# q of two early chunks turned in full tiles, their x in rows of tokens, first k and v loads in longer rows

## The chip, the cores and the metric

The kernel runs on one core of one Trainium2 chip. The metric is device time in microseconds (us), the median of several runs; less is better. TensorE multiplies, VectorE and ScalarE work element by element, GpSimd does small odd pieces (here a power), and SyncE issues every DMA.

## What is computed

Attention without softmax, then a two-layer feed-forward product with an odd nonlinearity. There are 8 batches of 8 heads, 576 tokens and 64 values a head; 4608 tokens of width 512 go through the second part, with 2048 hidden units.

```python
kv = np.einsum('bhsd,bhse->bhde', k, v)
out = np.einsum('bhsd,bhde->bhse', q, kv)
rms = np.sqrt(np.mean(out * out, axis=-1, keepdims=True) + 1e-06)
x = (out / rms * g_norm)          # then (tokens, heads * 64)
h = x @ w_in
g = h * np.cos(h)
return (g @ w_out).astype(np.float32)
```

q, k, v and g_norm are 32-bit floats. The two weight matrices come as 64-bit floats, and the kernel itself turns them into 32-bit pairs (a high and a low part).

## The kernel before, in words

The tokens are cut into 9 chunks of 512 (CH), the heads into 4 pairs (p), and the 2048 hidden units into 16 blocks j of 128. For each chunk and each pair a tile x, with the 128 values of the pair on the partitions and 512 tokens beside each other, is made from q and kv; it is split into a high and a low part (xhi, xlo).

A **step** is one chunk and one block j. Its first stage (stage1_part, line 683) makes h in one PSUM bank from four pairs, three products each (xhi with the high and the low weights, xlo with the high ones); act_part (line 708) makes g = h cos h on ScalarE and VectorE and splits it; the second stage (stage2_part, line 744) adds 4 x 3 products with w_out's block to four accumulators (acc0 to acc3). The order of the steps is in `segments` (line 245): chunk 0 with blocks 0 to 4, chunk 1 with blocks 0 to 6, chunk 0 with 5 to 15, chunk 1 with 7 to 15, and then the chunks 2 to 8 whole. What chunks 0 and 1 have added up at the first break goes out to memory and is added again later.

Each weight block (wi j for the first layer, wo j for the second) is loaded once, 512 KB, and converted by w_part (line 629): two or three operations on ScalarE (sg, wi or wo, sometimes m) and three or four on VectorE (m, sg, sg, and the low part). It then stays in its slot of wpool. The slots of the blocks needed last are lent (line 807) to the early loads of k, v and q and to kv_front, the 32-bit kv of batches 0 and 1; the lent block is loaded when the borrower is done.

Chunks 0 and 1 (FRONT = 2) are made in another way than the later ones, in plain 32-bit products:

- kv_loads_front and kv_load (lines 318 to 333) load k and v of a pair to 96 partitions, 6 tokens of 64 values in a row of 1536 bytes. kv_front_part (line 384) makes kv of the pair in 12 products, the two heads in the two halves of the columns, and copies the two 64 x 64 results.
- q_loads_front (line 351) puts q in rows of tokens, four tokens of a head side by side (1 KB a row). x_part (line 450) turns it with eight products by the identity, 64 columns wide (lines 460 to 464).
- chunk 0: four products with q as the stationary operand give x in rows of tokens (line 499); the sum of squares, the power on GpSimd, the scaling (lines 520 to 535), and then four transposes bring x to the needed form (line 537), from which xhi and xlo are read with g_norm as the factor.
- chunk 1: two products give x turned already (line 506), 448 and 64 tokens since the chunk covers two batches. The sums of squares are eight small products with `pair` (line 566), the factors are spread out by ScalarE and turned back by four transposes (line 580).

kv_split_part (line 434) splits batch 1's kv for chunk 2, pair by pair; chunks from 2 on use kv_hi and kv_lo.

The order of instructions on every engine is fixed when the program is made, by the planner `Order` (line 52). Every piece of work yields what it waits for, its cost on an engine and a priority; the planner takes the piece that can start first, and among those the lowest priority. Priorities come from `due(i)` (line 258), a guess at when step i is done. DMA is an engine of the planner with a cost of its own for each load (1.9 for k and v of a pair, 0.85 for q, 1.5 for a weight block), starting at 1.0, and a load counts as landed 2.0 later (DMA_LAT). The loads are issued by SyncE in that order. Engines run strictly in the planned order, so a piece planned too early blocks what stands behind it. The loads of the front and their priorities are in lines 819 to 838:

```python
t = due(begin[c]) - 32 + 3 * p if c else -100.0 + p
load(1.9, t, [kv_in[c, p]], kv_loads_front(c, p, lend(2, [kv_used[c, p]])))
```

Lines 227 to 231 multiply zeros 28 times before any data are there.

Of the kernel before, what the change touches and what calls it, by code (L numbers as in the profile page):

```python
# [19 lines left out]
P = 128  # L20
EPS = 1e-6
# [126 lines left out]
def tile_kernel(  # L148
# [23 lines left out]

    FRONT = 2

# [59 lines left out]
    pair = const.tile([P, 2], F32, name="pair")  # L234
    pool.memset(pair, 0.0)
    for j in range(2):
        pool.memset(pair[j * D:(j + 1) * D, j:j + 1], 1.0)
# [7 lines left out]
    segments = [(0, 0, 5), (1, 0, 7), (0, 5, 16), (1, 7, 16)]  # L245
# [24 lines left out]

# [58 lines left out]
    def kv_loads_front(b, p, tags):  # L329

        def issue():
            kv_load(b, p, *(wpool.tile([P, 2, SI, D], F32, name=f"{kind}{j}") for kind, j in tags))
        return issue
# [17 lines left out]
    def q_loads_front(c, p, tag):  # L351

        def issue():
# [3 lines left out]
            for b, s0, o0, n in chunk_parts(c):  # L357
                nc.sync.dma_start(  # L358
                    out=qn[o0 // NTT:(o0 + n) // NTT, :, :, :],
                    in_=q[b, 2 * p:2 * p + 2, s0:s0 + n, :].rearrange("h (r a) d -> r h a d", a=NTT))  # L360
# [23 lines left out]
    def kv_front_part(b, p, prio):  # L384
        yield "wait", [kv_in[b, p]]
        yield "take", t_psa, prio
        bank = yield "take", t_bank, prio
        _, end = yield "run", [("PE", 1.0)], prio
        ps = ps_tile(bank)
        kt, vt = kv_tiles.pop((b, p))  # L390
        for i in range(SI):
            for j in range(2):
                pe.matmul(
                    out=ps[j * D:(j + 1) * D, 0:D], lhsT=kt[0:SP, j, i, :], rhs=vt[0:SP, j, i, :],
                    start=(i == 0), stop=(i == SI - 1))
        sched.fire(kv_used[b, p], end)
        e, end = yield "run", [("ACT", 0.41, 0.0), ("DVE", 0.45, 0.3)], prio
        for j in range(2):
            r = slice(j * D, (j + 1) * D)
            copy(e, kv_front[r, b, p, j * D:(j + 1) * D], ps[r, 0:D])  # L400
# [33 lines left out]
    def kv_split_part(b, p, prio):  # L434

        yield "wait", [kv_done[b, p]]
        yield "run", [("ACT", 0.29)], prio
        act.copy(out=kv_hi[:, b % 2, p, :], in_=kv_front[:, b, p, :])
        _, end = yield "run", dve_only(P), prio
        dve.tensor_tensor(  # L440
            out=kv_lo[:, b % 2, p, :], in0=kv_front[:, b, p, :], in1=kv_hi[:, b % 2, p, :].bitcast(F32),
            op=ALU.subtract)
        sched.fire(kv_split[b, p], end)
# [6 lines left out]
    def x_part(c, p, prio):  # L450
        yield "wait", [q_in[c, p]]
        front = c < FRONT
        yield "take", t_two, prio
        if front:
            yield "take", t_psa, prio
            bank = yield "take", t_bank, prio
            _, _ = yield "run", [("PE", 0.9)], prio
            qn = q_tiles.pop((c, p))
            ps_t = ps_tile(bank)
            for a in range(NTT):  # L460
                for j in range(2):
                    pe.matmul(
                        out=ps_t[j * D:(j + 1) * D, a * P:(a + 1) * P], lhsT=qn[:, j, a, :], rhs=ident,
                        start=True, stop=True)
        else:
            yield "take", t_qT
            _, end = yield "run", [("DVE", dve_us())], prio
            qT = at.tile([P, CH], F32, name="qT", bufs=1)
            dve.transpose(out=qT, in_=q_tiles.pop((c, p)).rearrange("p a b -> p (a b)"))
            sched.give(t_q, end)  # L470
        if front:
            e, end = yield "run", copiers(), prio
            qT = at.tile([P, CH], F32, name="m")
            copy(e, qT, ps_t[:, 0:CH])
            give_ps(bank, end)
        else:
            yield "run", [("ACT", act_us())], prio
            qhi = at.tile([P, CH], F32R, name="m")
            qlo = at.tile([P, CH], F32R, name="sg")
            act.copy(out=qhi, in_=qT)  # L480
            _, end = yield "run", dve_only(CH), prio
            dve.tensor_tensor(out=qlo, in0=qT, in1=qhi.bitcast(F32), op=ALU.subtract)
            sched.give(t_qT, end)
        parts = chunk_parts(c)
        yield "wait", [kv_done[b, p] if front or b >= FRONT else kv_split[b, p] for b, _, _, _ in parts]
# [6 lines left out]
        pe_us = sum(0.88 * n / 512 if front else 3 * max(0.11, (n + 32) / 2400) for _, _, _, n in parts)  # L492
        _, end = yield "run", [("PE", pe_us)], prio if front else -1.0
        ps = ps_o.tile([P, DM], F32, name=f"acc{acc}") if c == 0 else ps_tile(bank)
        for b, s0, o0, n in parts:
            if c == 0:

                for a in range(NTT):
                    pe.matmul(
                        out=ps[:, a * P:(a + 1) * P], lhsT=qT[:, a * P:(a + 1) * P], rhs=kv_front[:, b, p, :],  # L500
                        start=True, stop=True)
                continue
            if front:
                out_r, q_r = (
                    t[:, 0:CH].rearrange("p (a r) -> p a r", a=NTT)[:, :, o0 // NTT:(o0 + n) // NTT] for t in (ps, qT))
                pe.matmul(out=out_r, lhsT=kv_front[:, b, p, :], rhs=q_r, start=True, stop=True)
                continue
# [11 lines left out]
        if c == 0:  # L519
            heads = lambda t: t.rearrange("p (n d) -> p n d", d=D)  # L520
            yield "run", [("DVE", dve_us())], prio
            ms = small.tile([P, 2 * NTT], F32, name="ms")
            dve.tensor_reduce(out=ms, in_=heads(sq), axis=AX.X, op=ALU.add)
            _, end = yield "run", [("DVE", 0.1)], prio
            sched.give(t_s1, end)
            dve.tensor_scalar(out=ms, in0=ms, scalar1=EPS, scalar2=None, op0=ALU.add)
            yield "run", [("POOL", 1.4)], prio
            rinv = small.tile([P, 2 * NTT], F32, name="rinv")
            pool.tensor_tensor(out=rinv, in0=ms, in1=mhalf[:, 0:2 * NTT], op=ALU.pow)
            yield "take", t_r, prio  # L530
            yield "run", [("DVE", dve_us())], prio
            x = ew.tile([P, CH], F32, name="r")
            dve.tensor_tensor(
                out=heads(x), in0=heads(ps[:, 0:CH]),
# [52 lines left out]
        else:  # L587
# [12 lines left out]
            for e in range(4):  # L600
                act.copy(out=swp[32 * (e ^ 1):32 * (e ^ 1) + 32, :], in_=part[32 * e:32 * e + 32, :])
# [293 lines left out]
```

## Time and profile before

| | us |
|---|---|
| median of 3 runs | 883.26 (881.87 to 884.6) |
| the profiled execution | 880.51 |
| its span, first to last instruction | 878.7 |
| TensorE busy | 866.5 (99%) |
| VectorE busy | 595.1 (68%) |
| ScalarE busy | 509.0 (58%) |
| GpSimd busy | 101.0 (11%) |

The profile is of one execution; its times are microseconds from the start of the span. PE is TensorE's multiplying, PEld its loading of the stationary operand, DVE is VectorE, ACT ScalarE, POOL GpSimd, SP SyncE. Nearly every instruction is recorded by one helper, so all have line 197 (L197), and groups are told apart by tiles: `bank` and `acc` are PSUM, and a tile of wpool shows the name of its slot, so early k, v, q and kv_front appear as `wi` or `wo`. One 32-bit product appears as two records (x8 for four products), one transpose as one. The busy time of products overlaps with the next ones, so that the price of a piece of TensorE work is read from start to start.

### The profile page before, as it was taken

The numbers are of one execution on the slowest core, as the hardware profiler recorded it, in microseconds if no ns is written. First come the engines' busy times: TensorE is split into PE (matmuls) and PEld (weight loads), VectorE is DVE, ScalarE is ACT, GpSimd is POOL, SyncE is SP. The second block draws the span as 40 slices with busy tenths as digits, with TensorE's granted clock in tenths as the row PEclk, the third lists the DMA queues.
The fourth block names the chain that finished last, engine by engine and source line by source line (L and its number), as shares of the span: only waits on it lengthen the run. The fifth ranks groups of instructions, "written<-read, shape, count | busy, mean of one in ns | idle before, by whom it ended". The sixth has DMA issues, their size and how long they took to land.

```text
span 878.7 us, 12282 instructions
## 1 busy us (share of the span) xinstructions
PE 866.5 (99%) x4648; PEld 718.4 (82%) x4648; DVE 595.1 (68%) x973; ACT 509.0 (58%) x972; POOL 101.0 (11%) x49
## 2 busy tenths in 40 slices
PE   7999999999999999999999999999999999999998
PEld 6878888888888888888888888888888888888886
DVE  2888989788677657765766567755766667654553
ACT  3788888556555556455655565545555555545444
POOL 2220000013021102110112011110211012100000
PEclk9999999999999999999999999999999999999999
DMA  9996020471422031302220042203000110001001
GB/s 261 306 366 194 1 73 0 125 192 31 122 44 41 7 90 37 67 13 54 73 67 13 0 115 64 28 1 114 13 13 13 25 48 1 1 1 48 1 1 48
DMA packets 94603, 59.52 MB, mean 68 GB/s; under 512 B 63312, under 2 KB 85840, under 8 KB 94544
## 3 DMA queue, kind: packets, MB, share of 16 engines
q1 hardware_dynamic: 94544, 58.74, 24.6%
q8 instruction: 36, 0.59, 0.3%
q14 instruction: 23, 0.19, 0.1%
HBM read 47.19 MB, written 11.53 MB: 67 GB/s over the span
## 4 chain that ended last, share of the span: by engine, by line
PE 96%; DMA 2%; ACT 1%; SPq 0%; issue 0%; DVE 0%; ACTq 0%
PE bank L197 51%; PE acc L197 45%; DMA wi<-in_moe_w_in_dram 1%; DMA out_dram<-ob 1%; DMA wo<-in_q_dram 1%; ACT ob L197 0%; SPq L320 0%; DVE sg L197 0%; ACT m L197 0%; ACT s L197 0%; DVE r L197 0%; ACT r L197 0%; SPq L358 0%; ACT ghi L197 0%; ACTq L197 0%
## 5 line engine op out<-in xcount | busy, mean ns | idle before, releaser
L197 PE MATMUL acc<-wo,ghi 128*128 128x512 f32 x1152 | 356.6, 391 | 0.2
L197 PE MATMUL bank<-xhi,wi 128*128 128x512 f32 x1088 | 337.8, 392 | 0.7 <-ACT m L197 0.7
L197 PEld LDWEIGHTS acc<-wo,ghi 128*128 128x128 f32 x1152 | 215.1, 188 | 45.7 <-ACT ob L197 0.6
L197 ACT ACTIVATE r<-r 128x512 f32<-128x512 f32 x288 | 181.5, 630 | 118.3 <-DVE r L197 114.8
L197 PEld LDWEIGHTS bank<-xhi,wi 128*128 128x128 f32 x1088 | 202.5, 188 | 42.8 <-ACT m L197 0.9
L197 PE MATMUL acc<-wo,glo 128*128 128x512 f32 x576 | 224.3, 389 | 0.0
L197 PE MATMUL bank<-xlo,wi 128*128 128x512 f32 x544 | 211.9, 389 | 0.0
L197 POOL TENSOR_TENSOR rinv<-ms,mhalf 128x16 f32<-128x16 f32 (+1 forms) x36 | 98.2, 2727 | 658.2 <-DVE ms L197 658.2
L197 DVE SCALAR_TENSOR_TENSOR r<-ki,bank 128x512 f32<-128x512 int32 x144 | 98.7, 685 | 85.5 <-ACT ki L197 84.4
L197 ACT ACTIVATE ki<-bank 128x512 int32<-128x512 f32 x144 | 85.8, 596 | 108.4 <-PE bank L197 106.2
L197 DVE SCALAR_TENSOR_TENSOR r<-r,bank 128x512 f32<-128x512 f32 x144 | 98.6, 685 | 72.4 <-ACT r L197 72.1
L197 PEld LDWEIGHTS acc<-wo,glo 128*128 128x128 f32 x576 | 108.1, 188 | 22.8
L197 DVE TENSOR_TENSOR glo<-r,ghi 128x512 fp32r<-128x512 f32 x144 | 98.3, 683 | 33.3 <-ACT ghi L197 32.4
L197 PEld LDWEIGHTS bank<-xlo,wi 128*128 128x128 f32 x544 | 102.1, 188 | 21.4
L197 ACT CAST ghi<-r 128x512 fp32r<-128x512 f32 x144 | 89.0, 618 | 48.1 <-DVE r L197 47.6
L197 DVE SCALAR_TENSOR_TENSOR r<-ki,r 128x512 f32<-128x512 int32 x144 | 98.7, 685 | 2.3
L197 ACT ACTIVATE s<-bank 128x512 f32<-128x512 f32 x32 | 19.2, 599 | 31.4 <-PE bank L197 31.4
L197 DVE STREAM_TRANSPOSE qT<-s 128x512 f32<-128x512 f32 x28 | 19.9, 710 | 18.7 <-ACT s L197 18.6
L197 DVE STREAM_TRANSPOSE s<-rinv 128x512 f32<-128x512 f32 x28 | 19.8, 708 | 16.3 <-POOL rinv L197 16.3
L197 ACT COPY swp<-part 32x16 f32<-32x16 f32 x112 | 22.6, 202 | 8.3 <-DVE part L197 6.7
L197 ACT CAST xhi<-s 128x512 fp32r<-128x512 f32 x32 | 19.7, 618 | 11.5 <-DVE s L197 11.3
L197 ACT ACTIVATE ob<-acc 128x512 f32<-128x512 f32 x31 | 18.2, 598 | 7.9 <-PE acc L197 5.4
(93 smaller groups left out, 544.8 us busy)
## 6 DMA issues: line engine op xcount, KB each, us to landing
wi<-in_moe_w_in_dram SPq DMA_DIRECT2D x16, 512.0 KB, 9.8
wo<-in_moe_w_out_dram SPq DMA_DIRECT2D x16, 512.0 KB, 8.7
out_dram<-ob SPq DMA_DIRECT2D x31, 256.0 KB, 2.1
kt<-in_k_dram SPq DMA_DIRECT2D x24, 288.0 KB, 4.0
vt<-in_v_dram SPq DMA_DIRECT2D x24, 288.0 KB, 4.6
qb<-in_q_dram SPq DMA_DIRECT2D x32, 48.0 KB, 2.3
wi<-in_k_dram SPq DMA_DIRECT2D x5, 288.0 KB, 6.2
wo<-in_v_dram SPq DMA_DIRECT2D x5, 288.0 KB, 9.2
```

The lines of the kernel that those rows point to most:

```text
L197: return lambda *a, **kw: tc.keep_in_program_order(f(*a, **kw))
```

## The change

1. q of chunks 0 and 1 is seen as tiles of 128 tokens by (two tokens of a head, 64 values) and is turned by four full transposes for a pair of heads instead of eight half-wide products. For that kv_front becomes one tile for each batch, with the kv of every head twice, in both halves of the diagonal (four copies for a pair instead of two).
2. Chunk 1 is made like chunk 0, in rows of tokens: six products (128 columns each) instead of two; two of the six are for the 64 tokens that still belong to batch 0 and write 32 rows. Then the sum of squares on VectorE, the power, the scaling and four transposes, as chunk 0 does. The products with `pair`, the spreading of the factors and their transposes go. x_front_part does this for both chunks; x_part keeps what chunks 2 to 8 need, unchanged. Chunk 1's q is loaded with two tokens in a row (512 bytes) in three pieces, and its output rows follow.
3. k and v of batch 0 are loaded to 128 partitions, 9 tokens in a row (2304 bytes), and multiplied in 9 x 2 products of 64 rows.
4. kv_split_part takes all pairs at once, in two copies and two subtractions.
5. The plan: segments of 4, 8, 12 and 8 steps, other due times, weight loads 4 earlier in priority, a table `haste` that moves single loads and pieces (wo1 and the k and v of pair 1 of batch 1 far ahead, q of pair 0 of chunk 0 behind the other pairs' q, k and v of its pairs 2 and 3 behind that), 34 products with zeros instead of 28, 22 lent slots instead of 21.

```diff
-    for _ in range(28):
+    for _ in range(34):
...
-    segments = [(0, 0, 5), (1, 0, 7), (0, 5, 16), (1, 7, 16)]
+    segments = [(0, 0, 4), (1, 0, 8), (0, 4, 16), (1, 8, 16)]
...
-        return 24.0 + STEP * i + 0.8 * min(i, 14)
+        return 24.0 + STEP * i + 1.6 * min(i, 14)
...
+    def front_rows(c):
+        if c == 0:
+            return [(0, 0, P, 0), (0, 0, P, 1)]
+        return [(1, 0, P, 0), (1, 0, P, 1), (0, 0, (S - CH) // 2, 0)]
...
+            kt, vt = (wpool.tile([P, SF, D], F32, name=f"{kind}{j}") for kind, j in tags)
+            for t, src in ((kt, k), (vt, v)):
+                nc.sync.dma_start(out=t, in_=src[b, 2 * p:2 * p + 2].rearrange("h (p i) d -> (h p) i d", i=SF))
...
+        n = SI if b else SF
+        for i in range(n):
+            for j, r in enumerate(heads):
+                lhs, rhs = (t[0:SP, j, i, :] if b else t[r, i, :] for t in (kt, vt))
+                pe.matmul(out=ps[r, 0:D], lhsT=lhs, rhs=rhs, start=(i == 0), stop=(i == n - 1))
...
+            for r in heads:
+                copy(e, kv_front[b][r, 2 * p + j, r], ps[heads[j], 0:D])
...
+        yield "wait", [kv_done[b, p] for p in range(NP)]
...
+        qn = q_tiles.pop((c, p)).rearrange("p j (m s) d -> p (j m) (s d)", s=2)
+        ps_t = ps_tile(bank)
+        for n in range(NTT):
+            pe.transpose(out=ps_t[:, n * P:(n + 1) * P], in_=qn[:, n, :], identity=ident)
...
+        by_token = ps.rearrange("p (a j d) -> p a j d", j=2, d=D)
+        for b, r0, r1, m in todo:
+            for j in range(2):
+                o = (2 * j + m) * P
+                pe.matmul(
+                    out=by_token[r0:r1, 2 * m:2 * m + 2, j, :], lhsT=qT[:, o + r0:o + r1],
+                    rhs=kv_front[b][:, 2 * p + j, :], start=True, stop=True)
...
-        prio = due(i + 2) - STEP
+        prio = due(i + 2) - 8.0
...
-    lent, slots = {}, sorted(need, key=lambda x: (need[x], x))[-10 * FRONT - 1:]
+    lent, slots = {}, sorted(need, key=lambda x: (need[x], x))[-11 * FRONT:]
...
+    haste = {
+        ("load kv", 0, 2): 2.5, ("load kv", 0, 3): 3.5, ("load kv", 1, 1): -98.4,
+        ("load q", 0, 0): 3.5, ("load q", 1, 2): 10.0,
+        ("load", "wi", 3): 10.0, ("load", "wo", 0): 10.0, ("load", "wo", 1): -130.0,
+        ("kv", 0, 3): -10.0, ("x", 1, 0): -2.0, ("x", 1, 2): -20.0, ("x", 1, 3): -20.0, ("wi", 1): 10.0,
+    }
...
+        (pool if b else dve).memset(kv_front[b], 0.0)
...
+            load(2.4 if c else 1.9, t, [kv_in[c, p]], kv_loads_front(c, p, lend(2, [kv_used[c, p]])))
...
+            load(1.1 if c else 0.85, t, [q_in[c, p]], q_loads_front(c, p, key))
...
-        load(1.5, due(need[key]) - 10, [w_in[key]], w_loads(key), wait=lent.get(key, ()))
+        t = due(need[key]) - 14 + haste.get(("load",) + key, 0.0)
+        load(1.5, t, [w_in[key]], w_loads(key), wait=lent.get(key, ()))
```

The scaling of chunk 1 is the code of chunk 0, lines 515 to 556, with the bank given back at its end.

## Rows read from the trace of the kernel before

**Rows 1.** The page, engine shares: busy us, share of the span, instructions.
```profile
PE 866.5 (99%) x4648; PEld 718.4 (82%) x4648; DVE 595.1 (68%) x973; ACT 509.0 (58%) x972; POOL 101.0 (11%) x49
```

**Rows 2.** The page, chain that ended last, share of the span by engine.
```profile
PE 96%; DMA 2%; ACT 1%; SPq 0%; issue 0%; DVE 0%; ACTq 0%
```

**Rows 3.** Stretches: PE, PEld, DVE, ACT, POOL busy (instructions), granted clock, DMA share, GB/s.
```profile
26.07:62.50 36.43, 35.32 (x286) 27.99 (x284) 29.91 (x57) 29.55 (x59) 6.64 (x4) 1.00 1.03 341
60.00:160.00 100.00, 100.00 (x448) 82.85 (x448) 90.25 (x150) 82.67 (x152) 1.64 (x1) 1.00 0.25 80
```

**Rows 4.** Timeline of TensorE: start, us, engine, operation, out<-in, shapes [idle before].
```profile
15.36 0.92 PE L197 MATMUL bank<-wi,wo 96*64 96x64 f32 x24
19.19 2.08 PE L197 MATMUL acc<-wo,m 128*128 128x128 f32 x8 [2.91 <-ACT m L197]
...
26.07 0.71 PE L197 MATMUL bank<-xhi,wi 128*128 128x512 f32 x2
...
46.71 0.62 PE L197 MATMUL acc<-wo,ghi 128*128 128x512 f32 x2
```

**Rows 5.** Timelines of ScalarE and VectorE: first operation on wi0, low halves of wi0, wo0.
```profile
17.98 0.69 ACT L197 ACTIVATE sg<-wi 128x512 f32<-128x512 f32 x1 [3.81 <-DMA wi<-in_moe_w_in_dram]
...
23.20 0.68 DVE L197 TENSOR_TENSOR wi<-sg,wi 128x512 fp32r<-128x512 f32 x1
...
39.72 0.69 DVE L197 TENSOR_TENSOR wo<-sg,wo 128x512 fp32r<-128x512 f32 x1
```

**Rows 6.** Stretches as in rows 3, about the first big product.
```profile
16.28:19.19 2.91, 0.00 (x0) 0.00 (x1) 1.21 (x3) 1.22 (x3) 0.00 (x0) 0.84 1.11 303
19.19:25.00 5.81, 5.81 (x51) 5.47 (x52) 4.68 (x10) 3.50 (x9) 3.69 (x2) 0.50 1.10 262
```

**Rows 7.** Timeline of TensorE, pieces of the early attention and what follows them.
```profile
9.46 1.16 PE L197 MATMUL acc<-wo,m 128*128 128x128 f32 x8
...
10.55 1.09 PE L197 MATMUL bank<-ident,wo 128*64 128x128 f32 x16
...
29.86 1.14 PE L197 MATMUL bank<-m,wo 128*128 128x64 f32 x4
30.93 1.09 PE L197 MATMUL bank<-ident,wo 128*64 128x128 f32 x16
31.95 0.73 PE L197 MATMUL bank<-kt,wi 128*128 128x512 f32 x2
...
33.44 0.60 PE L197 MATMUL acc<-ident,r 128*128 128x128 f32 x4
33.88 0.95 PE L197 MATMUL bank<-pair,s 128*128 128x2 f32 x8
34.69 0.71 PE L197 MATMUL bank<-xhi,wi 128*128 128x512 f32 x2
...
35.91 0.39 PE L197 MATMUL bank<-vt,wi 128*128 128x512 f32 x1
36.23 0.92 PE L197 MATMUL bank<-wo,wi 96*64 96x64 f32 x24
```

**Rows 8.** Packets in the windows 15 to 20, 45 to 50 and 182 to 190 us.
```profile
DMA packets 1371, 1.51 MB, mean 302 GB/s; under 512 B 78, under 2 KB 1371, under 8 KB 1371
q1 hardware_dynamic: 1371, 1.51, 110.1%
...
DMA packets 1145, 1.90 MB, mean 380 GB/s; under 512 B 59, under 2 KB 889, under 8 KB 1145
q1 hardware_dynamic: 1145, 1.90, 105.9%
...
DMA packets 3076, 1.78 MB, mean 223 GB/s; under 512 B 2258, under 2 KB 2562, under 8 KB 3076
q1 hardware_dynamic: 3076, 1.78, 78.8%
```

**Rows 9.** Groups by shape from 0 to 65 us: count, busy us, mean ns, idle before.
```profile
L197 DVE TENSOR_REDUCE ms<-s 128x8 f32<-128x512 f32 x4 | 2.7, 682 | 10.2 <-ACT s L197 10.2
L197 ACT COPY s<-rinv 128x512 f32<-128x512 f32 x4 | 2.5, 617 | 2.5 <-POOL rinv L197 2.5
L197 ACT COPY wo<-bank 64x64 f32<-64x64 f32 x16 | 3.3, 206 | 4.9 <-PE bank L197 4.5
```

More of the change, by code (lines that the diff above doesn't have):

```diff
@@ L432, in kv_part, with kv_split_part @@
             sched.fire(kv_done[b, p], end)
[L434 to L443, printed above, removed]
+    def kv_split_part(b, prio):
+        yield "wait", [kv_done[b, p] for p in range(NP)]
+        for j in range(2):
+            r = slice(j * D, (j + 1) * D)
+            src = kv_front[b].rearrange("p (n j) d -> p n j d", j=2)[r, :, j, r]
+            yield "run", [("ACT", act_us(NP * D))], prio
+            act.copy(out=kv_hi[r, b % 2, :, r], in_=src)
+            _, end = yield "run", [("DVE", dve_us(NP * D))], prio
+            dve.tensor_tensor(
+                out=kv_lo[r, b % 2, :, r], in0=src, in1=kv_hi[r, b % 2, :, r].bitcast(F32), op=ALU.subtract)
+        for p in range(NP):
+            sched.fire(kv_split[b, p], end)
@@ L446, in x_tokens, with x_front_part @@
     def x_tokens(c, p):
         return t_kv if c == 0 and p >= 2 else t_x
-    def x_part(c, p, prio):
+    def x_front_part(c, p, prio):
         yield "wait", [q_in[c, p]]
-        front = c < FRONT
         yield "take", t_two, prio
[L454 to L485, printed above, removed]
@@ L491, in x_part @@
             bank = yield "take", t_bank, prio
-        pe_us = sum(0.88 * n / 512 if front else 3 * max(0.11, (n + 32) / 2400) for _, _, _, n in parts)
-        _, end = yield "run", [("PE", pe_us)], prio if front else -1.0
+        _, end = yield "run", [("PE", 1.6 if c else 0.95)], prio
         ps = ps_o.tile([P, DM], F32, name=f"acc{acc}") if c == 0 else ps_tile(bank)
-        for b, s0, o0, n in parts:
[L496 to L507, printed above, removed]
+        by_token = ps.rearrange("p (a j d) -> p a j d", j=2, d=D)
@@ new lines, in x_front_part @@
+        yield "run", [("POOL", 1.4)], prio
+        rinv = small.tile([P, 2 * NTT], F32, name="rinv")
+        pool.tensor_tensor(out=rinv, in0=ms, in1=mhalf[:, 0:2 * NTT], op=ALU.pow)
+        yield "take", t_r, prio
+        yield "run", [("DVE", dve_us())], prio
+        x = ew.tile([P, CH], F32, name="r")
+        dve.tensor_tensor(
+            out=heads(x), in0=heads(ps[:, 0:CH]),
+            in1=rinv.rearrange("p (n o) -> p n o", o=1).broadcast_to([P, 2 * NTT, D]), op=ALU.mult)
+        _, end = yield "run", [("PE", 0.5)], prio
@@ new lines, in x_front_part @@
+        for a in range(NTT):
+            pe.transpose(out=ps[:, a * P:(a + 1) * P], in_=x[:, a * P:(a + 1) * P], identity=ident)
+        sched.give(t_r, end)
+        t_slot = x_tokens(c, p)
+        yield "take", t_slot, prio
+        yield "run", [("ACT", act_us() + 0.08)], prio
+        if t_slot is t_kv:
+            xhi, xlo = (
+                kvp.tile([P, 2, SI, D], F32R, name=n).rearrange("p h i d -> p (h i d)")[:, 0:CH]
+                for n in ("kt", "vt"))
+        else:
+            xhi, xlo = (xpool.tile([P, CH], F32R, name=n) for n in ("xhi", "xlo"))
@@ new lines, in x_part @@
+        yield "take", t_qT
+        yield "run", [("DVE", dve_us())], prio
+        sqT = at.tile([P, CH], F32, name="qT", bufs=1).rearrange("p (a b) -> p a b", b=32)
+        dve.transpose(out=sqT.rearrange("p a b -> p (a b)"), in_=sq)
+        _, end = yield "run", [("DVE", dve_us())], prio
+        part = small.tile([P, TB], F32, name="part")
+        dve.tensor_reduce(out=part, in_=sqT, axis=AX.X, op=ALU.add)
+        sched.give(t_s1, end)
+        sched.give(t_qT, end)
+        yield "run", [("ACT", 0.8)], prio
@@ new lines, in x_part @@
+        swp = small.tile([P, TB], F32, name="swp")
+        for e in range(4):
+            act.copy(out=swp[32 * (e ^ 1):32 * (e ^ 1) + 32, :], in_=part[32 * e:32 * e + 32, :])
+        yield "run", [("DVE", 0.17)], prio
+        ms = small.tile([P, TB], F32, name="ms")
+        dve.scalar_tensor_tensor(out=ms, in0=part, scalar=EPS, in1=swp, op0=ALU.add, op1=ALU.add)
+        yield "run", [("POOL", 2.6)], prio
+        rinv = small.tile([P, TB], F32, name="rinv")
+        pool.tensor_tensor(out=rinv, in0=ms, in1=mhalf, op=ALU.pow)
```

238 lines of the change are left out of this document (108 added, 130 removed).

## The prediction

> **What bounds it now.** I read the page's engine shares first: TensorE is busy in 99% of the span [rows 1], and the chain that ended last is TensorE for 96% of its length [rows 2]. So a microsecond counts only where TensorE works, waits or is slow. From 60 to 160 us it never waits [rows 3], and from there on the kernel repeats itself over chunks that the change leaves alone. What is left is the front. The TensorE timeline shows where the stream of the big MoE products begins: at 26.07 us [rows 4]. Before that lies a wait from 16.28 to 19.19 us: the product of the third pair needs a ScalarE copy, and that copy stands behind ScalarE's first conversion of the weight tile wi0, whose data are there at 17.98 us [rows 4, 5]. The granted clock falls during the wait and is 0.50, the lower level (1.2 GHz), from 19.19 to 25 us [rows 6]. From 26.07 to 62.5 us the rest of the early attention is mixed into the MoE products, and TensorE idles 36.43 - 35.32 = 1.1 us [rows 3]. So the end = T1 (start of the big products, 26.07) + early attention still to do after T1 + idle after T1 + a part that does not change. I go through the change by those terms.
>
> **TensorE work after T1.** Chunk 1's four pairs lie behind T1. Prices are starts minus starts.
> - Turning q: eight half-wide products, 30.93 to 31.95 = 1.02 us [rows 7]. They become four full transposes; four such of x take 33.44 to 33.88 = 0.44. -0.58 a pair.
> - x: two products, 29.86 to 30.93 = 1.07. They become six of 128 columns; four of that size take 9.46 to 10.55 = 1.09, so six take 1.63. Two of the six write only 32 rows, a change of array tile at each end. The nearest row for such a change: the half-wide kv product starts 0.32 after the product ahead of it (35.91 to 36.23), where the stream's pace is 100/448 = 0.22 [rows 3, 7]. 0.1 a change, two changes: 1.83. +0.76 a pair.
> - Sums of squares by products with "pair", 33.88 to 34.69 = 0.81, go to VectorE: -0.81. The four transposes of the spread factors (0.44) go, four of x (0.44) come: 0.
>
> Together -0.63 a pair, **-2.5 us** for four. The Trainium skill (TensorEngine Tiling (Array Packing), Key Properties) says that changing the tiling mode drains TensorE. If each of the eight changes cost a whole 0.27 product instead of 0.1, the sum would be -1.1; the row of 0.32 bears out a cost, but only the small one.
>
> The twelve products of kv of pair (1, 1), together 0.92 [rows 7], move ahead of T1, since their load is hastened by 98.4 to stand right behind chunk 0's: **-0.9**. Batch 0's kv takes 18 smaller products instead of 12, at 0.92/12 some 0.5 us more a pair, but before T1, in time in which TensorE waits for transfers (it has 12 to 13 us of work in the first 23); nothing, and at most +1.8 if that cover is gone. Six more warming products on zeros, of 28, lie in the same wait.
>
> **T1.** It hangs on wi0's landing (17.95), then on its conversion, done at 23.88 [rows 5], then on the queue in front of it at half clock. Time for each packet of a DMA engine: from 15 to 20 us 5 x 16 x 1.101/1371 = 64 ns at a mean of 1101 B; from 45 to 50 us 5 x 16 x 1.059/1145 = 74 ns at 1659 B; where rows of 128 B rule (182 to 190 us) 33 ns at 580 B [rows 8]. The line through the first two gives 62 ns for 1 KB, 72 for 1536 B, 85 for 2304 B and 117 for 4 KB, estimates. Batch 0's eight tiles of k and v go from 1536 packets of 1536 B to 1024 of 2304 B: (1536 x 72 - 1024 x 85)/16 = -1.5 us; between 0 and -2.0 (same time a packet). New ahead of wi0 are wo1 (128 packets of 4 KB, +0.9) and k, v of pair (1, 1) (384 x 72/16 = +1.7). So wi0 lands 1.1 later, at some 19.1 (18.6 to 20.6). On the other side ScalarE is planned to wait for it only at 19.9 by the kernel's own sums of transfer costs, behind the copies of chunk 0, so the wait of 2.9 us for the copy goes, and the chunk-0 products that ran at half clock from 19.19 run before. The conversion's five steps take 3.4 us alone (0.69, 0.68, 0.69, 0.61, 0.68 by the operations of its kind), 5.9 as they stood. T1 is 22.5 to 26; I take 23.5, nearer the short end since nothing of chunk 0 but the last pair's scaling stands in its way: **-2.6**. What comes late next is that last pair, whose k and v now come after all q.
>
> **Idle after T1.** Now 1.1 us; unknown after. Below: it vanishes, -1.1. Above: see the third case. I take **+0.8**, since wo0 is later (below).
>
> **Side work.** VectorE gains a reduction a pair (0.68) on chunk 1 [rows 9], +2.7 us, and some copies; ScalarE loses the copy of the spread factors and the cast of x (0.62 each), -4.9, and gets twice the kv copies (3.3 more, shared with VectorE). The split of batch 1's kv is four operations in place of eight. Nothing as long as VectorE's idle time covers it: 6.5 us from 26.07 to 62.5, 9.75 from 60 to 160 [rows 3]. kv_front is two tiles now, one weight slot more is lent, and the second memset is on GpSimd, idle then: nothing, or a late wo14 (second case). The steps are cut 4, 8, 12, 8 instead of 5, 7, 11, 9: the same products, with eight weight pairs instead of seven wanted by step 11, and sixteen by step 23 instead of 22: nothing by itself.
>
> Sum: -2.5 - 0.9 - 2.6 + 0.8 = **-5.2 us**. The profiled execution took 880.51 us (span 878.7 and 1.8 around it), so 875.3 for that one; the median of the runs is 883.26, 2.75 above it, and I forecast the median, 878.0.
>
> **The cases.**
> 1. The front shrinks and stays shrunk: 874 to 880.5, likeliest 878.0. Chance 0.65. For it: TensorE has no wait after 62.5 us in which a gain could be lost now.
> 2. VectorE gives the gain back. Sixteen weight pairs must be converted in the first two chunks, and VectorE is busy 90.25 of 100 us from 60 to 160 [rows 3]. Coming 5.2 us earlier with 2.7 more work asks for 7.9 of its idle time. If only half of the 9.75 can be used, because the order of instructions is fixed and the idle time lies between waits, TensorE stands still for 7.9 - 4.9 = 3.0: 881.0, no measurable change. For it: wo14's slot now waits for the whole split of batch 1. Against it: part of the work fits in the 6.5 us before. Chance 0.19.
> 3. Slower: TensorE starves between T1 and the first product of the second stage. That one needs wo0, converted by 40.4 us and first used at 46.71 [rows 4, 5], 6.3 us of slack. wo0's load now stands behind k and v of pairs (1, 2) and (1, 3), a q and wo1 too, 1.96 MB; at 302 GB/s [rows 8] that is 6.5 later, less 1.5 for batch 0's rows, and chunk 1's q comes in 512 B rows, twice the packets: by the line between 33 ns at 580 B and 64 at 1101 B about 30 ns each, nothing more; at the same time a packet (64) 512 x 64/16 = 2.0 a load less 1.0, over three loads 3 us. So wo0 is 5.0 to 8.0 later, while its use is wanted some 4 earlier: late by 3 to 6 unless its conversion is done faster than before. If late by 5.5, TensorE idles so long and runs at half clock afterwards as it does from 19.19 to 25 (2.9 lost of 5.8 us [rows 6]): +8.4 - 5.2 = +3.2, 886.5. It decides from the point where wo0's low half is done later than about 44 us. Against it: the conversion's steps need only 3.4 us alone, and steps 3 to 5 of the first stage can be run ahead. Chance 0.16. By the Trainium skill (DMA: Bandwidth & Descriptors, Specifications) rows of 512 B are long enough for line rate, so that the q loads would cost nothing more. The trace has no 512 B load, but speaks against line rate at that length, as rows of 1659 B carry 22 B per ns and engine and rows of 1101 B 17; by the rule this case would be late by 3, not 6: 3 + 2.9 - 5.2, near 884.
>
> **The numbers.** 0.3% or 2.65 us is about what a measurement of this kernel can tell from no change. Case 1 is faster by more (0.65), case 2 within (0.19), case 3 slower (0.16). The range leaves out about 0.07 below (T1 at 22.5 and no idle: -2.5 - 0.9 - 3.6 - 1.1 = -8.1, and a kv or transposing row cheaper than priced: 873.5) and 0.12 above, within the third case: 873.5 to 885.0; case 1 alone is 874 to 880.5.
>
> **What would show it.** The first big product near 23.5 us; no TensorE wait of 2.9 us before it and less time at clock 0.50; four full transposes in about 0.44 us for q; six x products in about 1.8; sums on "pair" gone; wo0's low half before 44; k and v of batch 0 in 1024 packets, landing earlier; VectorE at about 93% from 60 to 160 with TensorE still without a wait. It is wrong if T1 is at 26 or later, if TensorE idles more than 3 us between T1 and 62.5, or if waits of TensorE for VectorE appear after 60 us.

## The result and the profile after

The changed kernel takes **873.11 us** (median of 4 runs, 872.91 to 873.9); the kernel before took 882.57 beside it (4 runs, 881.23 to 884.6). The ratio is 0.9893, interval 0.9871 to 0.9914: 9.5 us faster, where 878.0 and a gain of 5.2 were forecast. The direction was right; the forecast gain was 4 us too small, and 873.11 lies just below the range. The profiled execution took 873.28 (span 871.5).

The page of the changed kernel, engine shares and the first line of the chain, answers to [rows 1, 2]:

```profile
PE 860.1 (99%) x4606; PEld 714.5 (82%) x4606; DVE 597.0 (69%) x974; ACT 511.8 (59%) x979; POOL 99.4 (11%) x47
...
PE 96%; DMA 3%; SPq 0%; ACT 0%; issue 0%; ACTq 0%
```

TensorE still sets the end; it is busy 6.4 us less, and the span is 7.2 shorter. The TensorE timeline of the changed kernel (columns as in [rows 4]) at the places that the prediction named:

```profile
7.83 0.66 PE L199 MATMUL bank<-ident,wi 128*128 128x128 f32 x4
9.95 0.66 PE L199 MATMUL bank<-ident,wi 128*128 128x128 f32 x4 [1.46 <-DMA wi<-in_q_dram]
10.89 2.05 PE L199 MATMUL acc<-wo,m 128*128 128x128 f32 x16 [0.28 <-ACT m L199]
12.87 1.26 PE L199 MATMUL bank<-wi,wo 64*64 64x64 f32 x36
16.10 1.26 PE L199 MATMUL bank<-wo,wi 64*64 64x64 f32 x36 [1.97 <-DMA wo<-in_v_dram]
17.30 0.66 PE L199 MATMUL bank<-ident,wi 128*128 128x128 f32 x4
...
21.35 0.92 PE L199 MATMUL bank<-wi,wo 96*64 96x64 f32 x24
22.20 0.66 PE L199 MATMUL bank<-ident,wi 128*128 128x128 f32 x4
24.28 1.68 PE L199 MATMUL bank<-wo,m 128*128 128x128 f32 x12 [1.43 <-ACT m L199]
25.90 0.66 PE L199 MATMUL acc<-ident,r 128*128 128x128 f32 x4
26.48 0.92 PE L199 MATMUL bank<-wo,wi 96*64 96x64 f32 x24
27.33 0.73 PE L199 MATMUL bank<-xhi,wi 128*128 128x512 f32 x2
...
33.14 1.61 PE L199 MATMUL bank<-wo,m 128*128 128x128 f32 x12
34.67 0.73 PE L199 MATMUL bank<-xhi,wi 128*128 128x512 f32 x2
...
36.18 0.60 PE L199 MATMUL bank<-ident,wo 128*128 128x128 f32 x4
36.54 0.71 PE L199 MATMUL bank<-kt,wi 128*128 128x512 f32 x2
...
44.00 0.74 PE L199 MATMUL acc<-wo,ghi 128*128 128x512 f32 x2
```

The first big product (T1) starts at 27.33, later than before (26.07), not at 23.5. But pair (1, 1) has gone through its kv, its turn and its x by then (21.35, 22.20, 24.28). The first second-stage product starts at 44.00 (46.71). No wait is longer than 1.97 us; the one of 2.91 is gone. wi0 is later: the timelines of ScalarE and of VectorE, to be held against [rows 5], show its first operation at 21.60 and wo0's low half at 39.84; wo1, now among the first loads, is converted from 9.24 to 13.6:

```profile
9.24 0.69 ACT L199 ACTIVATE sg<-wo 128x512 f32<-128x512 f32 x1 [1.68 <-DMA wo<-in_moe_w_out_dram]
...
21.60 0.70 ACT L199 ACTIVATE sg<-wi 128x512 f32<-128x512 f32 x1 [0.30 <-DMA wi<-in_moe_w_in_dram]
```

```profile
9.25 0.43 DVE L199 TENSOR_SCALAR m<-wo 128x512 int32<-128x512 uint32 x1 [1.83 <-DMA wo<-in_moe_w_out_dram]
...
12.91 0.69 DVE L199 TENSOR_TENSOR wo<-sg,wo 128x512 fp32r<-128x512 f32 x1 [0.74 <-ACT wo L199]
...
39.84 0.68 DVE L199 TENSOR_TENSOR wo<-sg,wo 128x512 fp32r<-128x512 f32 x1
```

Stretches of the changed kernel (columns as in [rows 3]):

```profile
19.00:25.00 6.00, 4.57 (x54) 4.17 (x55) 4.50 (x9) 5.46 (x13) 2.01 (x1) 1.00 1.11 277
27.33:56.34 29.01, 28.48 (x198) 23.46 (x195) 26.65 (x47) 24.98 (x52) 7.26 (x5) 1.00 1.01 340
4.00:80.00 76.00, 69.97 (x575) 58.49 (x573) 61.57 (x110) 59.79 (x127) 14.19 (x9) 1.00 0.99 307
60.00:160.00 100.00, 100.00 (x443) 82.81 (x442) 89.11 (x149) 80.73 (x148) 0.00 (x0) 1.00 0.26 79
```

and one of the kernel before, which was not shown yet:

```profile
4.00:80.00 76.00, 69.31 (x587) 57.12 (x586) 53.99 (x99) 53.13 (x109) 14.01 (x8) 0.96 1.00 302
```

The granted clock from 19 to 25 us is 1.00 where it was 0.50 [rows 6]. From 27.33 to 56.34 TensorE idles 0.53 us. From 60 to 160 us TensorE has no wait and VectorE is at 89.11. The rows from 4 to 80 us hold nearly the whole story: after a hundred big products the changed kernel is 6.8 us ahead (61.3 against 68.1), and its span is 7.2 shorter. 76 less the busy time is TensorE's **idle** time, 6.69 before and 6.03 after. The **half-clock cost** is busy time times what the granted clock lacks to 1, summed over windows of half a microsecond: 2.96 before and 0.00 after. What is left of the span is **work at full clock**. All times of the next table are us, worked out so from each kernel's rows, with T1 beside them (the labels are those of the experiments below):

| profiled execution | span | idle | half-clock cost | the rest: work | T1 |
|---|---|---|---|---|---|
| before | 878.7 | 6.7 | 3.0 | 869.0 | 26.1 |
| e1, before again | 882.2 | 6.1 | 4.8 | 871.2 | 27.4 |
| e4, before, wi0's conversion planned later | 886.9 | 8.5 | 5.9 | 872.5 | 31.5 |
| e8, before's operations, new plan | 884.9 | 9.9 | 6.1 | 868.9 | 33.0 |
| after | 871.5 | 6.0 | 0.0 | 865.5 | 27.3 |
| e10, after again | 870.9 | 4.2 | 1.7 | 865.0 | 27.3 |
| e11, 28 zero products | 872.1 | 6.8 | 0.0 | 865.3 | 27.4 |
| e12, q ahead of wo1 | 874.4 | 6.1 | 3.3 | 865.0 | 30.8 |
| e5, short rows | 875.1 | 5.6 | 6.1 | 863.4 | 29.7 |
| e6, pair (1, 1) not early | 876.9 | 8.6 | 2.6 | 865.7 | 31.3 |
| e7, wo1 not early | 881.0 | 11.1 | 3.4 | 866.5 | 32.3 |
| e3, no `haste` | 877.7 | 8.1 | 3.4 | 866.2 | 24.5 |
| e9, after's operations, old plan | 876.8 | 8.1 | 1.7 | 867.0 | 25.6 |
| e2, half-wide turns | 873.1 | 2.8 | 0.0 | 870.3 | 27.2 |

The four kernels with the old operations have 870.4 us of work on the mean, the nine with the new ones (without e2) 865.5: **4.9 less**, though a single one is known to some 2 us only. Idle and half clock together are 10.3 in the two executions of the kernel before and 6.3 in the three of the new one (after, e10 and e11, whose zeros change nothing): **4.0 less**. Together 8.9; the medians say 9.5 here and 8.8 in e10. T1 does not put the kernels in order: the earliest, 24.5, belongs to e3, whose span is 6.2 us longer than that of the changed kernel.

### The profile page after: what moved, and what is told of

It reads as the page before. It is cut to its first block, busy times and chain, and to the rows that moved or that the text cites. A ratio compares the mean times of both kernels' runs of the same rounds, so it can differ in the third digit from the quotient of the medians.

```text
span 871.5 us, 12217 instructions
## 1 busy us (share of the span) xinstructions
PE 860.1 (99%) x4606; PEld 714.5 (82%) x4606; DVE 597.0 (69%) x974; ACT 511.8 (59%) x979; POOL 99.4 (11%) x47
## 4 chain that ended last, share of the span: by engine, by line
PE 96%; DMA 3%; SPq 0%; ACT 0%; issue 0%; ACTq 0%
PE bank L199 51%; PE acc L199 45%; DMA wo<-in_v_dram 1%; DMA wi<-in_moe_w_in_dram 1%; DMA wi<-in_v_dram 1%; DMA wi<-in_q_dram 1%; DMA out_dram<-ob 0%; SPq L342 0%; ACT ob L199 0%; ACTq L199 0%
## 5 line engine op out<-in xcount | busy, mean ns | idle before, releaser
L199 POOL TENSOR_TENSOR rinv<-ms,mhalf 128x16 f32<-128x16 f32 (+1 forms) x36 | 96.0, 2667 | 652.8 <-DVE ms L199 652.8
L199 PEld LDWEIGHTS acc<-wo,glo 128*128 128x128 f32 x576 | 108.1, 188 | 22.8
L199 ACT COPY swp<-part 32x16 f32<-32x16 f32 x112 | 22.6, 202 | 10.2 <-DVE part L199 8.6
L199 ACT ACTIVATE ob<-acc 128x512 f32<-128x512 f32 x31 | 18.3, 597 | 6.4 <-PE acc L199 4.2
L199 DVE SCALAR_TENSOR_TENSOR sg<-sg,m 128x512 int32<-128x512 int32 x32 | 21.7, 686 | 0.1
```

Source lines behind the costliest of these rows:

```text
L199: return lambda *a, **kw: tc.keep_in_program_order(f(*a, **kw))
```

## The experiments

What each theory says stands in the texts quoted. Differences between variants are taken between their medians. The kernel before, run beside each, moved between 881.30 and 882.57 itself; by the ratios to it the changed kernel stands at 0.9893 and 0.9905 (e10), and small differences come out larger (e2 2.3 to 3.4 us instead of 2.0, e5 1.1 to 2.1 instead of 0.9, e6 5.0 to 6.1 instead of 4.6).

**The two ends again.** e1 is the kernel before, unchanged; e10 the changed one.

> The kernel before, unchanged, to see what differs between its own runs (881.2 to 884.6 so far, while the changed kernel keeps within 1.0). Theory A (the stretch at half clock behind the 2.9 us wait of TensorE varies from run to run): this execution too shows the wait near 16 us and a stretch at clock 0.50 after it, and runs with a lower mean clock are longer; a stretch of 5.8 us more or less moves the time by about 2.9. Theory B (the spread has nothing to do with the clock): mean clocks are alike within 0.001 while times differ by 2 us or more.

882.27 (10 runs, 880.89 to 884.11) against 881.47 (19 runs), ratio 1.0012, 1.0 to 1.0024. This profiled execution took 883.99, 3.5 more than the first one, and its stretches show where the front differs:

```profile
20.00:25.00 5.00, 4.66 (x42) 4.43 (x44) 4.05 (x10) 2.90 (x8) 2.54 (x2) 0.50 1.11 247
25.00:30.00 5.00, 5.00 (x67) 4.45 (x63) 3.27 (x7) 2.85 (x7) 1.54 (x1) 0.83 1.09 300
...
40.00:50.00 10.00, 8.89 (x49) 6.88 (x48) 8.93 (x17) 9.01 (x18) 1.64 (x1) 0.86 1.05 384
```

The stretch at the lower level (1.2 GHz, 0.50) comes again after the wait for the copy (3.46 us here), and a second one follows waits of 0.42 and 0.69 us near 45 us. Over 62 runs of the kernel before, the 16 with the lowest mean granted clock (up to 0.995) take 883.3 us on the mean, the other 46 take 881.3: a lower clock goes with some 2 us of their scatter of 5, as theory A had it.

> The changed kernel, unchanged. Theory A (it keeps the full clock through the start, so its runs lie close): median 872.5 to 874, all within 1.5. Theory B (it has good and bad executions as the variants without some of the moves have, 872 to 877): a spread of 3 or more and some mean clocks under 0.996.

873.45 (6 runs, 871.94 to 874.66), ratio 0.9905, 0.9886 to 0.9924. The gain repeats; the spread of 2.7 lies between the two theories. Here too a stretch falls below full clock (0.73 from 10 to 15 us). It costs 1.7 us, but the idle time is 1.8 less than in the first execution, and the span is not longer.

**The operations and the plan, crossed.** e9 has all new operations and loads with the old segments, due times, load costs and priorities, and no `haste`; e8 the old operations with the new plan.

```diff
-    segments = [(0, 0, 4), (1, 0, 8), (0, 4, 16), (1, 8, 16)]
+    segments = [(0, 0, 5), (1, 0, 7), (0, 5, 16), (1, 7, 16)]
...
-    haste = {
...
+    haste = {}
...
-        t = due(need[key]) - 14 + haste.get(("load",) + key, 0.0)
+        t = due(need[key]) - 10 + haste.get(("load",) + key, 0.0)
```

> The changed kernel's operations and loads under the plan of before (steps cut 5, 7, 11, 9, old due times and transfer costs, no table of moves, 28 products with zeros). With the runs so far (both old 881.4, old operations under the new plan 886.7, both new 873.1) it closes a square. Theory A (the new operations save 3.6 us of TensorE work wherever they stand): 877 to 878.5. Theory B (each plan fills the start only with the operations that it was made for, the saved work turns into waits and half clock): 880 to 884.

880.3 (877.97 to 880.9), ratio 0.9977, 0.9963 to 0.9991: the operations alone bring 1.9 us (0.8 to 3.3 by the interval), and the plan is needed for the rest, as theory B had it. The TensorE timeline shows waits for the conversion of a wo block, then the stretch around them:

```profile
54.69 0.49 PE L199 MATMUL acc<-wo,ghi 128*128 128x512 f32 x1 [1.28 <-ACT wo L199]
55.57 0.50 PE L199 MATMUL acc<-wo,ghi 128*128 128x512 f32 x1 [0.38 <-DVE wo L199]
```

```profile
50.00:60.00 10.00, 7.57 (x36) 5.21 (x34) 9.18 (x17) 7.55 (x14) 2.72 (x2) 1.00 1.06 397
```

> The kernel before with the changed plan alone: steps cut 4, 8, 12, 8, the new due times, earlier weight loads, the table of moved loads and pieces, 34 products with zeros; the operations of the front as before. Theory A (the plan makes the gain whatever the operations): 874 to 878. Theory B (plan and operations are only worth something together, since the plan fills the time with work whose length it counts on): 879 to 883. Theory C: slower than before, the plan being made for other lengths.

886.71 (885.38 to 889.82), ratio 1.0071, 1.0046 to 1.0096: 5 us slower, theory C. The timeline shows a wait for a load and the second stage held up; from 30 to 35 us, behind the first wait, the granted clock is 0.50:

```profile
29.33 1.55 PE L197 MATMUL bank<-wi,wo 96*64 96x64 f32 x24 [4.63 <-DMA wi<-in_v_dram]
...
53.70 0.49 PE L197 MATMUL acc<-wo,ghi 128*128 128x512 f32 x1 [1.51 <-ACT wo L197]
```

So the square is 882 (old, old), 887 (old operations, new plan), 880 (new, old) and 873 (new, new). The two halves don't add: -2 and +5 alone, -9 together. e9's profiled execution has the work of the new kernels within 1.5 us, and 9.8 us of idle and half clock, as much as the kernel before (9.7 and 10.9): under the old plan the waits stay. That execution was 1.7 us faster than e9's median, so that the rows don't show where the rest of its saved work went.

**What in the plan.** e3 empties `haste`; e7 takes only wo1's entry out of it, e6 only that of k and v of pair (1, 1).

```diff
-        ("load", "wi", 3): 10.0, ("load", "wo", 0): 10.0, ("load", "wo", 1): -130.0,
+        ("load", "wi", 3): 10.0, ("load", "wo", 0): 10.0,
```

> The changed kernel with an empty table of moved loads and pieces; all else as changed. Theory A (cheaper work makes the gain, the moves only fill waits at the start): at most 3 us slower, 873 to 876. Theory B (the order of the first loads makes the gain: without k and v of batch 1's pair 1 and wo1 ahead, TensorE has nothing to do before the first big product): 5 us or more slower, 878 to 882, and a wait or a stretch at clock 0.50 is back before the first big product.

881.41 (879.47 to 882.54), ratio 0.9998, 0.9986 to 1.001: without the table nothing is left of the gain, as theory B had it, and e3, which keeps the rest of the new plan, is no faster than e9 with the old one (880.3). Its timeline of TensorE:

```profile
19.71 1.24 PE L199 MATMUL bank<-wo,wi 96*64 96x64 f32 x24 [2.88 <-DMA wo<-in_v_dram]
41.21 0.92 PE L199 MATMUL bank<-wo,wi 96*64 96x64 f32 x24 [1.09 <-ACT m L199]
43.10 2.26 PE L199 MATMUL bank<-wo,m 128*128 128x128 f32 x12 [0.97 <-ACT wo L199]
```

> The changed kernel with wo1 loaded at its turn instead of fifth of all. Theory A (its early conversion uses idle ScalarE and VectorE time, 1.9 and 2.5 us, that is missed between 30 and 45): TensorE waits for ScalarE or VectorE between 30 and 45, 1 to 3 us slower. Theory B (its 512 KB hold up the loads of chunk 0 by some 1.4 us): 0.5 to 1.5 faster.

882.39 (878.54 to 883.78), ratio 0.9999, 0.9982 to 1.0016. With the rest of the table in place this one entry is worth 9.3 us, far beyond the 1 to 3 us of theory A. Shown are the timeline of TensorE; the first operation on a wo block on ScalarE in e7, and below it the changed kernel's first on wo0; the low halves of e7's first wo blocks on VectorE; then the stretch from 50 to 60 us of e7 and, below it, of the changed kernel:

```profile
14.78 1.26 PE L199 MATMUL bank<-wo,wi 64*64 64x64 f32 x36 [2.86 <-DMA wo<-in_v_dram]
...
32.31 1.19 PE L199 MATMUL bank<-xhi,wi 128*128 128x512 f32 x2
...
53.23 0.71 PE L199 MATMUL acc<-wo,ghi 128*128 128x512 f32 x2
...
58.02 0.63 PE L199 MATMUL bank<-ident,r 128*128 128x128 f32 x4 [1.79 <-DVE r L199]
```

```profile
45.26 0.67 ACT L199 ACTIVATE sg<-wo 128x512 f32<-128x512 f32 x1
```

```profile
35.32 0.67 ACT L199 ACTIVATE sg<-wo 128x512 f32<-128x512 f32 x1
```

```profile
51.03 0.68 DVE L199 TENSOR_TENSOR wo<-sg,wo 128x512 fp32r<-128x512 f32 x1
...
58.39 0.68 DVE L199 TENSOR_TENSOR wo<-sg,wo 128x512 fp32r<-128x512 f32 x1
```

```profile
50.00:60.00 10.00, 7.11 (x39) 5.21 (x38) 9.50 (x17) 8.23 (x16) 3.65 (x2) 1.00 1.06 397
```

```profile
50.00:60.00 10.00, 10.00 (x48) 8.24 (x47) 9.79 (x16) 9.44 (x19) 0.93 (x1) 1.00 1.06 396
```

Half of the loss is there before the stream begins: the first big product starts at 32.31 instead of 27.33, and from 4 to 33 us idle time and half-clock cost together are 10.2 us, where the changed kernel has 6.0. The second stage starts at 53.23 instead of 44.00, and from 45 to 60 us TensorE idles 2.9 us, where the changed kernel idles 0.0. This is not a late load: the first two wo blocks have landed by 35.7 us, and ScalarE takes up the first of them at 45.26; the changed kernel's wo0 lands at 35.3 and is taken up at 35.32. Nor is VectorE more crowded from 50 to 60 us (9.50 of 10, and 9.79 in the changed kernel). It is behind: from 4 to 45 us it is busy for 22.8 us in e7 and for 29.4 in the changed kernel, which converts wo1 from 9.2 to 13.6 us, when ScalarE and VectorE had stood still for 1.68 and 1.83 us.

The early load has a cost of about the size that theory B named, though the sum goes the other way: v of pairs (0, 2) and (0, 3) and wi0 land at 11.4, 16.0 and 21.6 us with it and at 10.3, 14.6 and 20.3 without. What e7 does not show is how much of the 9.3 us is wo1's conversion itself. With one entry less the planner orders all pieces anew: kv of pair (0, 3) now comes before that of (0, 2) (14.78 and 17.71), and wi0, landed earlier, has its low half done 3.1 us later.

> The changed kernel without the hastened loads of k, v and q of pair 1 of batch 1 (they fall back behind wi1). Theory A (this pair's kv, turn and x are what TensorE does in the time until wi0 is converted): wi0 lands some 2.5 us earlier, but TensorE waits before or just after the first big product, with a stretch at clock 0.50: 3 to 7 us slower, 876 to 880. Theory B (wi0 sets the start): 1 to 2.5 us faster.

877.72 (876.11 to 881.83), ratio 0.9962, 0.9938 to 0.9986: 4.6 us slower than the changed kernel, as theory A had it. wi0 lands 3.3 us earlier (18.3 against 21.6), and the first big product comes 4.0 later (31.30). Timeline, then the stretch that follows the second wait:

```profile
22.85 0.92 PE L199 MATMUL bank<-wo,wi 96*64 96x64 f32 x24 [1.79 <-DMA wo<-in_v_dram]
26.16 3.04 PE L199 MATMUL bank<-wo,m 128*128 128x128 f32 x12 [1.57 <-ACT m L199]
```

```profile
25.00:30.00 5.00, 3.84 (x16) 3.04 (x16) 2.54 (x5) 2.65 (x5) 1.64 (x1) 0.50 1.07 295
```

The pair's early load holds wi0 back; it gives TensorE work at 21 to 24 us that would otherwise be a wait, and x takes 3.04 us at the lower level instead of 1.68.

**wi0's conversion planned later, in the kernel before.** The prediction let the wait of 2.9 us go because ScalarE was planned to take wi0 later. e4 tries that by itself: it tells the planner that wi0 lands 2.5 us later, and the planner orders the rest around it.

```diff
+    LATE = 2.5
...
+        if key == ("wi", 0):
+            late = Event()
+            sched.fire(late, w_in[key].t + LATE)
+            yield "wait", [late]
```

> The kernel before, with only the planned landing of wi0 put 2.5 us later, so that the copies of chunk 0 stand ahead of its first conversion on ScalarE. Theory A (the wait of 2.9 us and the half clock are covered by wi0's late landing: the first big product cannot start before 24): 1 to 2.5 us faster than before, 880 to 881.5. Theory B (wait and half clock are on the path in full): 2.9 + 2.9 = 5.8 faster, near 876.8. Theory C (the plan is shifted and something else waits): no faster.

887.59 (885.31 to 888.63), ratio 1.0062, 1.0038 to 1.0086: 5 us slower, theory C; the first big product comes at 31.5. The wait for ScalarE's copy is gone, and a longer one for a load has its place, with the lower clock behind it (0.52 from 25 to 30 us):

```profile
24.78 1.55 PE L197 MATMUL bank<-wi,wo 96*64 96x64 f32 x24 [4.23 <-DMA wi<-in_v_dram]
```

**The pieces of work.** e2 turns q with half-wide products again, all else as changed.

```diff
-            pe.transpose(out=ps_t[:, n * P:(n + 1) * P], in_=qn[:, n, :], identity=ident)
+            for s in range(2):
+                pe.matmul(
+                    out=ps_t[s * D:(s + 1) * D, n * P:(n + 1) * P], lhsT=qn[:, n, s * D:(s + 1) * D], rhs=ident,
+                    start=True, stop=True)
```

> The changed kernel with each full transpose of q replaced by two half-wide products of the same data by the identity; same plan, same layout. Theory A (the gain is TensorE work taken out of the front): 1.02 - 0.44 = 0.58 us for a pair comes back, over four pairs of chunk 1 at least 2.3 and over all eight 4.6, so 875.4 to 877.7. Theory B (the gain is the plan and the clock, and the turns lie in waits): within 1 us of 873.1.

875.15 (874.71 to 876.15), ratio 0.9931, 0.9913 to 0.9949: 2.0 slower than the changed kernel, 2.3 to 3.4 by the ratios, near the lower end of theory A. The row from 4 to 80 us:

```profile
4.00:80.00 76.00, 73.16 (x664) 60.78 (x662) 59.84 (x107) 58.26 (x124) 14.23 (x9) 1.00 1.00 316
```

The work is 4.8 us more (870.3 against 865.5), 0.60 for each of the eight turns; idle time and half-clock cost together are 2.8, where the three executions of the changed kernel have 5.9 to 6.8. So a good part of the saved work lies where TensorE would have waited: three to six tenths of it by the medians and ratios, two thirds or more by the profiled executions. The full turn alone in the kernel before wasn't tried; it gives two tokens of one head, and so needs the doubled kv of item 1.

e5 gives batch 0 its 96 partitions and rows of 1536 bytes back (two conditions, and 12 products).

```diff
-            if b:
+            if True:
...
-        n = SI if b else SF
+        n = SI
```

> The changed kernel with k and v of batch 0 loaded and multiplied as before (96 partitions, rows of 1536 B, 12 products a pair); plan as changed. Theory A (longer rows save 1.5 us of transfer time at the start, and TensorE waits for these transfers): the first big product, at 27.33, comes 0.5 to 1.5 us later, 873.5 to 874.7. Theory B (transfers at the start are hidden by other waits, and the shorter products even help): within 0.5 of 873.1. Theory C (128 partitions carry much more than the packet count says): 876 or more.

874.04 (872.11 to 876.91), ratio 0.9917, 0.9889 to 0.9946: 0.9 slower than the changed kernel, with overlapping intervals, so that theory A is not told from theory B. In the profiled execution the first big product comes 2.4 us later (29.7), not 0.5 to 1.5. The transfers from 4.5 to 16 us show a difference, e5 and then the changed kernel:

```profile
DMA packets 2446, 3.20 MB, mean 278 GB/s; under 512 B 250, under 2 KB 2318, under 8 KB 2446
```

```profile
DMA packets 2721, 3.76 MB, mean 327 GB/s; under 512 B 296, under 2 KB 1946, under 8 KB 2720
```

The changed kernel moves 0.56 MB more in the same time, though e5's profiled execution was the slowest of its runs and has the most half-clock cost of all, 6.1 us.

**Two small ones.** e11 has 28 zero products instead of 34. e12 loads q of pair (0, 0) ahead of wo1, since a wait of 1.46 us for q stands at 9.95.

```diff
-        ("load q", 0, 0): 3.5, ("load q", 1, 2): 10.0,
-        ("load", "wi", 3): 10.0, ("load", "wo", 0): 10.0, ("load", "wo", 1): -130.0,
+        ("load q", 0, 0): 1.05, ("load q", 1, 2): 10.0,
+        ("load", "wi", 3): 10.0, ("load", "wo", 0): 10.0, ("load", "wo", 1): -129.9,
```

> The changed kernel with 28 products with zeros at the start instead of 34. Theory A (the last six keep TensorE at work until the first k and v are there at 4.85; without them the clock falls at the start): a stretch at clock 0.50 before 12 us in the profile, 0.5 to 2.5 us slower, spread wider. Theory B (they lie in a wait and change nothing): within 0.5 and the same spread.

873.23 (872.05 to 875.09), ratio 0.9904, 0.9885 to 0.9923: no effect, theory B.

> The changed kernel with the load of q of pair 0 put just ahead of wo1 instead of behind it, to shorten TensorE's wait of 1.5 us for it at 8.4. Theory A (what TensorE does in the start decides): the wait goes, but the pieces behind are held by the transfers of pairs 2 and 3 as before and wo1's conversion comes 0.6 later: within 0.5, or 0.5 to 1 faster. Theory B (the plan is balanced on the arrival of wo1): slower by 1 or more.

872.57 (871.78 to 876.23), ratio 0.9893, 0.9871 to 0.9914: not to be told from the changed kernel, as theory A allowed. The wait for q is gone, and waits of 2.9 and 1.8 us for ScalarE's copies stand in its place in the profiled execution, which was the slowest of the five (876.23).

## Why the prediction was right and wrong

- **The step that failed is the cut at T1**: "Chunk 1's four pairs lie behind T1", and "T1 is 22.5 to 26; I take 23.5". Pair (1, 1) had its kv, its turn and its x ahead of T1 (21.35, 22.20, 24.28), and T1 came at 27.33. By the prediction's own sign ("It is wrong if T1 is at 26 or later") it was wrong, and yet the kernel gained more than forecast. In both profiled executions 26 groups of three big products, 0.68 us each, are done at 62.49 and 56.34 us, 6.15 earlier. By the prediction's own terms: T1 +1.26 (forecast -2.6); early attention after T1 -6.8 (18.74 less 1.11 of idle time, down to 11.33 less 0.53), forecast -3.4 with kv of (1, 1); idle after T1 -0.6 (forecast +0.8). Attention that moves ahead of T1 delays T1 and shortens what follows. The sum of -6.1 comes near the forecast -5.2 only because errors of +3.9, -3.4 and -1.4 nearly cancel: that is luck. Another 1.05 of the 7.2 us lies behind 62.49, where the kernel before still has four transposes of the early attention, at 66.03; the rest of the miss is the step from the profiled execution to the median (last point).
- **How it came to miss T1.** wi0 was forecast at 19.1 and is first used at 21.60, as it lands; from there T1 took 5.7 us more, where 4.4 were allowed. The moves in the table add up: an entry for a pair's k and v moves its q as well. So q of pair (1, 1) stands ahead of wi0 in SyncE's queue too, 0.7 us that stood in no term; wo1 took 1.9 us of the queue and k and v of (1, 1) 2.1, where 0.9 and 1.7 were forecast. The same reading error stands in the change as described above: q of pair (0, 0) stands behind wo1 and pair 1's q, but ahead of k, v and q of pairs (0, 2) and (0, 3). Nor do "k and v now come after all q" for the last pair: its q is loaded behind them.
- **Work set at nothing.** Chunk 0's cheaper turns stand in no term, and batch 0's dearer kv was booked as "nothing", because TensorE waits there anyway. Per piece, from starts: the turn 36.18 to 36.54 = 0.36 against 1.02 (e2: 0.60 saved each; 0.58 forecast, right); x 33.14 to 34.67 = 1.53 (1.83 forecast); kv of batch 0 16.10 to 17.30 = 1.20 against 26.48 to 27.33 = 0.85 for the old form. Over eight turns (-4.8), four x (1.53 - 1.07, +1.8), four sums (-0.81 each, -3.2) and four kv (+1.4) that is -4.8 of work, as the table's 4.9, where the sum had -2.5. By e2 such work is worth less than its length when it is saved by itself (2.0 to 3.4 us of 4.8). The rest of the gain goes with less idle time and half-clock cost (6.3 against 10.3 us), which neither the operations alone (e9) nor the plan alone (e8) has.
- **x's change of array tile.** Two products of the six write 32 rows. Chunk 0's eight full ones go from 10.89 to 12.87, 0.25 each, so that six take 1.49, and the two changes cost 0.02 each, not 0.1. The Trainium skill (TensorEngine Tiling (Array Packing), Key Properties) says that a change of tiling mode drains TensorE. By these rows a drain costs no more than that 0.02 us here.
- **Half clock.** It was counted inside T1, and only what it cost up to there. It cost 3.0 and 4.8 us in the two executions of the kernel before, 0.0, 1.7 and 0.0 in the three of the new one. In e1, e4 and e6 the stretches at 0.50 or 0.52 stand right behind waits of 1.6 to 4.2 us, and in e8 one behind a wait of 4.6. The wait alone doesn't decide: e1's second stretch follows waits of 0.42 and 0.69, while behind the changed kernel's waits of 1.46 and 1.97 the clock stayed at 1.00.
- **Batch 0's rows** were forecast as 1.5 us earlier transfers, and the direction is right (327 against 278 GB/s); e5 values it at 0.9 us of the end (1.1 to 2.1 by the ratios), hardly clear of the noise. By the Trainium skill (DMA: Bandwidth & Descriptors, Specifications) rows from 512 B on are at line rate, so that 1536 and 2304 B would not differ. By the Trainium skill (DMA: Bandwidth & Descriptors, Rules for kernel authors) 128 partitions, in loads of 1 MiB or more, give the best bandwidth. The two runs, with 288 KB a load, do differ, against the first and with the second. They don't tell row length from the number of partitions.
- **Case 2 fell.** VectorE was at 89.11 of 100 from 60 to 160 us, with TensorE at 100.00; it is not the bound. The forecast of 93% was wrong.
- **Case 3 didn't happen.** wo0 did land later, by 4.0 us (35.3 against 31.3; 5.0 to 8.0 were forecast), but it was taken up at once, and its low half came at 39.84, as before (39.72), ahead of the point of decision at 44. e7 has a low half at 51.03 and loses 9.3 us, near the 8.4 of this case, but in another way: there wo0 lay landed for some ten us before ScalarE took it up, and half the loss stands ahead of T1. That the number fits is chance. The early wo1, booked by the prediction only as a cost of 0.9 us, is what the gain hangs on.
- **The median.** The forecast moved the profiled execution's shift to the median. The spans differ by 7.2, the medians by 9.5: before's profiled execution (880.51) is faster than its median here by 2.1, the new one's (873.28) is at its own. So 2.3 us of the miss lie in the choice of the execution that the sum started from.

What stays open: how much of e7's 9.3 us is wo1's early conversion and how much the new order of all the other pieces (wo1's load ahead, with the rest of the table empty, wasn't run); how much of e5's small cost is rows and how much partitions; and what chunk 1 in rows of tokens and the joined split of kv are worth by themselves, since of the operations only the turn and batch 0's loads were taken back one by one.

## What to carry to other kernels

In a start that is planned in a fixed order, work taken from the bounding engine is worth only what the waits leave of it: change the operations and the order of loads and conversions together, and judge them crossed, not one after the other. Don't measure such a start by the moment its first big product begins (the earliest here, 24.5 us in e3, came with no gain), but by idle time, half-clock cost and work up to the same count of big products. A weight block loaded and converted in an early stretch where the element-wise engines wait can be worth far more than its transfer costs there: here 9.3 us for 1.9 us of the queue, with everything planned around it.

## What was not expected of the hardware

- One 512 KB load and its conversion, moved from between 28 and 59 us to the first 14, was worth 9.3 us together with the order that the planner makes around it (e7). The transfer rate from 10 to 15 us is 345 GB/s with it and 313 without.
- The same kernel's front differs between executions: e10 has 4.2 us idle and 1.7 of half-clock cost where the first execution has 6.0 and 0.0, with spans 0.6 us apart.
